# The order of the closing waits on the SP queue of a SwiGLU kernel

## The chip, the cores and the metric

The kernel runs on one core of one Trainium2 chip. The metric is the device time of one execution in microseconds, lower is better. Each timed execution also comes with the span of the core, from its first to its last recorded instruction; in the profiled executions the time is 1.8 to 2.0 us longer than the span.

Names: PE is TensorE's matmul pipeline, ACT is ScalarE, DVE is VectorE, POOL is GpSimd, SP is SyncE. SP computes nothing here; it issues most DMAs and does the closing waits. S[102] is semaphore number 102. A DMA raises its semaphore by 16 in sixteen updates; the last of the sixteen is called its landing.

## The reference, cut to what matters

```python
B, S, D, F = 1, 2048, 640, 1536          # all bfloat16
def reference(x, w_gate, w_up, w_down):
    g = jax.nn.silu(x @ w_gate)
    u = x @ w_up
    return (g * u) @ w_down
```

## The kernel before

The kernel works in four blocks of 512 rows: gate and up projection, SiLU on ACT, product on DVE, then the down projection in four pieces of 128 rows. At the start, eight matmuls on constants warm TensorE up while x is being loaded.

```python
    N_WARM = 8
    ...
    def warm(n):
        pw = psum.tile([P, S_BLK], f32, tag="gu", name="pw", bufs=4)
        for _ in range(n):
            nc.tensor.matmul(pw[:], lhsT=ones[:, 0:P], rhs=ones, start=True, stop=True)
    warm(N_WARM)
    ... # then the first blocks of x are transposed (pt), and the projections begin
```

The very last piece of output, stored in two parts by two queues:

```python
            nc.scalar.copy(ot[:, 0:DA], po_a[:])
            if not last:
                nc.scalar.copy(ot[:, DA:D], po_b[:])
                nc.sync.dma_start(out=out2[s0 : s0 + P, :], in_=ot[:])
            else:
                nc.sync.dma_start(out=out2[s0 : s0 + P, 0:DA], in_=ot[:, 0:DA])    # L172, raises S[100]
                nc.scalar.copy(ot[:, DA:D], po_b[:])
                nc.scalar.dma_start(out=out2[s0 : s0 + P, DA:D], in_=ot[:, DA:D])  # L174, raises S[102]
```

The end of the program is not in the source: leaving the tile context adds it. SP gets one drain that waits for eleven semaphores (eight of the DMAs, and those of DVE, ACT and POOL). Then comes a barrier of all engines, in which POOL gathers and releases; then POOL clears the semaphores; then comes a second barrier. The compiler does not leave the eleven waits in one instruction. It keeps the first of the list in the drain and puts the other ten into five semaphore-wait instructions ahead of it, paired from the two ends of what is left of the list, the outermost pair last. The built program of before has this order on SP (S[100] to S[108] without 101 are the DMAs, 109 is DVE, 110 ACT, 99 POOL):

```
1  wait   S[104], S[103]
2  wait   S[105], S[102]      <- S[102]: the store L174, the last to land
3  wait   S[106], S[100]      <- S[100]: the store L172
4  wait   S[107], S[109]
5  wait   S[108], S[110]
6  drain  S[99]
7  drain of the first barrier: S[97]==0, then raises S[96], for which POOL waits
```

The Trainium skill (Perfetto Trace Analysis, Identifying Dependency Chains) says that "instructions waiting on multiple engines may have EventSemaphore instructions inserted prior to the instruction with additional wait conditions". This program agrees: five of them were inserted ahead of the drain. Which semaphore lands in which of them is what the change is about.

Of the kernel before, what the change touches and what calls it, by code (L numbers as in the profile page):

```python
# [7 lines left out]


@with_exitstack  # L10
def kernel(
    ctx: ExitStack,
    tc: tile.TileContext,
    x: bass.AP,
# [5 lines left out]
    nc = tc.nc  # L20
# [153 lines left out]
                nc.scalar.dma_start(out=out2[s0 : s0 + P, DA:D], in_=ot[:, DA:D])  # L174


# [1 line left out]
_INS = ['x', 'w_gate', 'w_up', 'w_down']  # L178
_OUTS = [((1, 2048, 640), 'bfloat16')]
# [25 lines left out]
```

## Time and profile before

| | before |
|---|---|
| time, median of 3 runs | 167.04 us (166.79 to 167.18) |
| span of the profiled execution | 165.2 us |
| PE busy | 160.5 us, 97% of the span |
| issue of the last store L174 | 162.560 us |
| landing of S[100] / S[102] | 163.981 / 164.147 us |
| POOL's step of the first barrier | 164.496 us |
| clearing of the semaphores | 164.767 us |

The page of before, its busy times, and its chain of work that ended last:

```profile
PE 160.5 (97%) x890; PEld 80.3 (49%) x907; DVE 34.9 (21%) x52; ACT 43.5 (26%) x81; POOL 0.7 (0%) x6
...
PE 97%; issue 1%; DVE 0%; ACT 0%
```

TensorE is the limit for nearly the whole span, so the closing waits on SP can matter only in the tail, which is a different stage. The timeline of ACT from 161.5 us on (start, duration, what) shows where computing stops, and the DMA issues of the window from 162 to 165 us (size, then issue to landing in us) show what comes after it:

```profile
162.26 0.27 ACT L173 CAST ot<-po_b 128x128 bf16<-128x128 f32 x1
162.56 0.36 ACTq L174 DMA_DIRECT2D out_dram<-ot  x1
```

```profile
out_dram<-ot SPq DMA_DIRECT2D x1, 128.0 KB, 1.7
out_dram<-ot ACTq DMA_DIRECT2D x1, 32.0 KB, 1.6
```

From 162.56 us on, the core waits 1.6 us for a store of 32 KB and then closes down. The view of the source line to which the end of the program belongs (L200), SP only, lists its wait instructions with the shortest, median and longest duration in ns and the first and last start:

```profile
L200 SPq EVENT_SEMAPHORE  x7: 17/28/1472, 162.6 to 165.1; - x7
L200 SPq DRAIN  x3: 7/7/13, 164.4 to 164.7; - x3
```

One wait took 1472 ns, the others 17 to 28. That view does not say which one. The single records of the trace do (start in us, duration in ns):

```
162.629    28  SP    EVENT_SEMAPHORE  S[104] S[103]
162.698  1472  SP    EVENT_SEMAPHORE  S[105] S[102]     ends at 164.170
              (S[102] landed at 164.147)
164.204    28  SP    EVENT_SEMAPHORE  S[106] S[100]
164.268    28  SP    EVENT_SEMAPHORE  S[107] S[109]
164.329    28  SP    EVENT_SEMAPHORE  S[108] S[110]
164.394    13  SP    DRAIN            S[99]
164.464     7  SP    DRAIN            S[97]==0, raises S[96]
164.496    17  POOL  EVENT_SEMAPHORE  S[96]>=4
```

The second wait is the decisive one. When it ends, SP still has to walk through four instructions, three waits and a drain, whose conditions have been met (S[100] 0.17 us earlier, the others long before). It arrives at the barrier 0.29 us later, and everyone else is already there.

### The profile page before, as it was taken

How to read it: one execution, taken by the hardware profiler on the slowest of the kernel's cores; microseconds unless marked ns; L12 is line 12 of the kernel's file. 1: busy time of each engine (PE TensorE's matmuls, PEld its weight loads, DVE VectorE, ACT ScalarE, POOL GpSimd, SP SyncE). 2: the span in 40 equal slices, each digit the busy share in tenths (PEclk: the TensorE clock that was granted, in tenths of full speed). 3: DMA queues.
4: the chain of work that ended last, by engine and by line, in shares of the span. 5: the costliest groups of instructions: out<-in, count | busy, mean ns of one | idle time of the engine just before them, and what ended most of it. 6: DMA issues, size and time to landing. Idle time of an engine off the chain costs nothing.

```text
span 165.2 us, 2137 instructions
## 1 busy us (share of the span) xinstructions
PE 160.5 (97%) x890; PEld 80.3 (49%) x907; DVE 34.9 (21%) x52; ACT 43.5 (26%) x81; POOL 0.7 (0%) x6
## 2 busy tenths in 40 slices
PE   8999999999999999999999999999999999999992
PEld 2844444455644444455554444445654444445551
DVE  0433333300013333310003333330002233331000
ACT  3042222222332222223232222222232222222222
POOL 1000000000000000000000000000000000000000
PEclk9999999999999999999999999999999999999999
DMA  5999999801110000001110000001111000000121
GB/s 147 294 326 327 362 230 223 160 29 55 40 40 0 0 4 0 0 0 42 68 55 0 0 2 0 0 4 40 40 40 40 4 0 0 0 0 0 46 78 40
DMA packets 18906, 11.27 MB, mean 68 GB/s; under 512 B 9681, under 2 KB 18897, under 8 KB 18897
## 3 DMA queue, kind: packets, MB, share of 16 engines
q1 hardware_dynamic: 18096, 10.95, 24.2%
q10 hardware_dynamic: 800, 0.20, 0.5%
q8 instruction: 7, 0.11, 0.3%
q14 instruction: 3, 0.02, 0.0%
HBM read 6.55 MB, written 2.62 MB: 56 GB/s over the span
## 4 chain that ended last, share of the span: by engine, by line
PE 97%; issue 1%; DVE 0%; ACT 0%
PE pg L112 31%; PE pu L112 31%; PE po_a L150 25%; PE po_b L159 7%; PE pw L98 2%; PE pt L105 1%; DVE xT L108 0%; ACT ot L173 0%
## 5 line engine op out<-in xcount | busy, mean ns | idle before, releaser
L112 PE MATMUL pg<-xT,wg_sb 128*128 128x512 bf16 (+2 forms) x244 | 59.5, 371 | 0.4
L112 PE MATMUL pu<-xT,wu_sb 128*128 128x512 bf16 (+2 forms) x241 | 59.6, 375 | 0.2
L141 DVE TENSOR_TENSOR aT<-sg,pu 128x512 bf16<-128x512 f32 x48 | 33.0, 687 | 109.2 <-PE pu L112 108.0
L140 ACT ACTIVATE sg<-pg 128x512 f32<-128x512 f32 x48 | 28.7, 597 | 76.2 <-PE pg L112 76.2
L150 PE MATMUL po_a<-wd_sb,aT 128*128 128x512 bf16 x185 | 43.4, 379 | 0.3
L112 PEld LDWEIGHTS <-wu_sb 128*128 128x128 bf16 x245 | 23.7, 98 | 27.9
L112 PEld LDWEIGHTS <-wg_sb 128*128 128x128 bf16 x250 | 24.0, 98 | 27.2 <-issue 0.2
L150 PEld LDWEIGHTS <-aT 128*128 128x128 bf16 x192 | 18.3, 98 | 19.8
L167 ACT CAST ot<-po_a 128x512 bf16<-128x512 f32 x16 | 9.4, 585 | 40.4 <-PE po_a L150 38.0
L159 PEld LDWEIGHTS <-aT 128*128 128x128 bf16 x192 | 12.1, 98 | 3.8
L159 PE MATMUL po_b<-wd_sb,aT 128*128 128x128 bf16 x192 | 13.3, 220 | 0.1
L98 PE MATMUL pw<-const-bfloat16-1.0 128*128 128x512 bf16 x8 | 3.6, 625 | 0.8 <-PEq L189 0.8
L169 ACT CAST ot<-po_b 128x128 bf16<-128x128 f32 x15 | 4.0, 265 | 1.1
L108 DVE COPY xT<-pt 128x640 bf16<-128x640 bf16 x4 | 2.0, 490 | 5.8 <-PE pt L105 5.7
L105 PEld LDWEIGHTS <-x_sb 128*128 128x128 bf16 x20 | 2.0, 133 | 0.6 <-DMA x_sb<-in_x_dram 0.5
L105 PE MATMUL pt<-ident,x_sb 128*128 128x128 bf16 x20 | 2.2, 289 | 0.0
L98 PEld LDWEIGHTS <-const-bfloat16-1.0 128*128 128x128 bf16 x8 | 1.0, 137 | 2.4 <-issue 2.4
L140 ACT ACT_TABLE_LOAD x1 | 1.3, 1283 | 1.3 <-PEq L189 1.3
masks.py:199 POOL TENSOR_SCALAR_AFFINE_SELECT ident<-ident 128x128 bf16<-128x128 bf16 x1 | 0.3, 292 | 0.1
L173 ACT CAST ot<-po_b 128x128 bf16<-128x128 f32 x1 | 0.3, 265 | 0.0
masks.py:197 POOL MEMSET ident<- 128x128 bf16 x1 | 0.2, 204 | 0.3 <-POOLq L189 0.3
L189 POOL MEMSET const-bfloat16-1.0<- 128x1 bf16 x1 | 0.1, 101 | 0.0
(3 smaller groups left out, 0.3 us busy)
## 6 DMA issues: line engine op xcount, KB each, us to landing
out_dram<-ot SPq DMA_DIRECT2D x15, 160.0 KB, 1.8
wd_sb<-in_w_down_dram SPq DMA_DIRECT2D x1, 1920.0 KB, 12.5
wg_sb<-in_w_gate_dram SPq DMA_DIRECT2D x3, 480.0 KB, 7.0
wu_sb<-in_w_up_dram SPq DMA_DIRECT2D x3, 480.0 KB, 7.6
x_sb<-in_x_dram SPq DMA_DIRECT2D x1, 320.0 KB, 3.2
x_sb<-in_x_dram SPq DMA_DIRECT2D x2, 160.0 KB, 3.7
wg_sb<-in_w_gate_dram SPq DMA_DIRECT2D x1, 320.0 KB, 5.0
wu_sb<-in_w_up_dram SPq DMA_DIRECT2D x1, 320.0 KB, 5.5
```

The costliest lines, as they stand in the source:

```text
L98: nc.tensor.matmul(pw[:], lhsT=ones[:, 0:P], rhs=ones, start=True, stop=True)
L105: nc.tensor.transpose(out=pt[:, kd, :], in_=x_sb[:, c, kd * P : (kd + 1) * P], identity=ident[:])
L108: nc.vector.tensor_copy(out=xT[:, :, c * P : (c + 1) * P], in_=pt[:])
L112: nc.tensor.matmul(ps[:, c0:c1], lhsT=w_sb[:, kd, fc * P : (fc + 1) * P], rhs=xT[:, kd, sb * S_BLK + c0 : sb * S_BLK + c1], start=(kd == 0 ...
L140: nc.scalar.activation(sg[:], pg[:], ACT.Silu)
L141: nc.vector.tensor_tensor(out=aT[:, fc, s_sl], in0=sg[:], in1=pu[:], op=ALU.mult)
L150: nc.tensor.matmul(po_a[:], lhsT=aT[:, kf, s0 : s0 + P], rhs=wd_sb[:, kf, 0:DA], start=(kf == 0), stop=(kf == KF - 1),)
L159: nc.tensor.matmul(po_b[:], lhsT=aT[:, kf, s0 : s0 + P], rhs=wd_sb[:, kf, DA:D], start=(kf == 0), stop=(kf == KF - 1),)
L167: nc.scalar.copy(ot[:, 0:DA], po_a[:])
L169: nc.scalar.copy(ot[:, DA:D], po_b[:])
L173: nc.scalar.copy(ot[:, DA:D], po_b[:])
L189: nc = _bacc.Bacc("TRN2", target_bir_lowering=False, num_devices=1)
```

## The change

The intent is to put the semaphores that rise last at the end of SP's walk, so that the other waits are done while the last store is still landing. A function goes over the built program, notes for each semaphore the last instruction that raises it, and sorts the waits of the closing drain. The latest goes first in the list, because the compiler keeps the first of the list in the drain, which is executed last.

```diff
+def _wait_for_the_latest_last(nc):
+    raised = {}
+    for block in nc.main_func.blocks:
+        for k, ins in enumerate(block.instructions):
+            s = ins.sync_info
+            for u in (s.on_update if s is not None else []):
+                raised[u.id] = (block.name, k)
+    at = {b.name: n for n, b in enumerate(nc.main_func.blocks)}
+    ... # for each drain with more than two waits:
+                key = lambda w: (at[raised[w.id][0]], raised[w.id][1])
+                block.instructions[k] = mybir.InstDrain(
+                    ...
+                        on_wait=sorted(s.on_wait, key=key, reverse=True),
+                    ...
+                )
+
+def tile_standalone__swiglu_ffn__prompt_kernel(tc, *args):
+    _body(tc, *args)                     # the kernel of before
+    tc.close()
+    tc.compile()
+    _wait_for_the_latest_last(tc.nc)
```

The built program differs from before in SP's six closing instructions and nowhere else:

```
1  wait   S[109], S[106]
2  wait   S[105], S[107]
3  wait   S[104], S[108]
4  wait   S[103], S[100]
5  wait   S[99],  S[110]
6  drain  S[102]
7  drain of the first barrier
```

More of the change, by code (lines that the diff above doesn't have):

```diff
@@ L10, with _body @@
 @with_exitstack
-def kernel(
+def _body(
     ctx: ExitStack,
@@ L174, with kernel @@
                 nc.scalar.dma_start(out=out2[s0 : s0 + P, DA:D], in_=ot[:, DA:D])
+def _wait_for_the_latest_last(nc):
[6 more added lines that the diff above has]
+    at = {b.name: n for n, b in enumerate(nc.main_func.blocks)}
+    for block in nc.main_func.blocks:
+        for k, ins in enumerate(block.instructions):
+            s = ins.sync_info
+            if isinstance(ins, mybir.InstDrain) and s is not None and len(s.on_wait) > 2:
+                key = lambda w: (at[raised[w.id][0]], raised[w.id][1])
+                block.instructions[k] = mybir.InstDrain(
+                    name=ins.name,
+                    engine=ins.engine,
+                    is_reset_sema=ins.is_reset_sema,
+                    debug=ins.debug,
+                    sync_info=mybir.SyncInfo(
+                        on_wait=sorted(s.on_wait, key=key, reverse=True),
+                        on_update=list(s.on_update),
+                    ),
+                )
+def kernel(tc, *args):
+    _body(tc, *args)
+    tc.close()
+    tc.compile()
+    _wait_for_the_latest_last(tc.nc)
 _INS = ['x', 'w_gate', 'w_up', 'w_down']
```

## The prediction

> **What bounds the kernel.** TensorE. The page gives PE busy 97% of a span of 165.2 us at a granted clock of 1.000, and the chain that ended last is 97% PE. The last po_b matmul's result comes at 162.24, the ACT copy L173 runs 162.26 to 162.53, and ACT issues the last store (L174) at 162.56. In the remaining 2.6 us nothing computes: the store lands, then come the closing waits and barriers. The change touches only those.
>
> **The tail, from the records of the end of the program (line L200, SP, and the DMA landings, us):**
> - Store L172 (S[100], issued by SP) has its 16th update at 163.981; store L174 (S[102], issued by ACT) at 164.147. The store before them landed by 161.07.
> - SP goes through five waits of two semaphores each and a drain with one. The second holds S[102]: it starts at 162.698, takes 1472 ns and ends at 164.170, 23 ns after the last landing.
> - Behind it stand waits whose semaphores have long risen: starts 164.204, 164.268, 164.329 (28 ns each), the drain at 164.394 (13 ns), and the barrier's drain at 164.464. Only then POOL goes on (164.496). ACT's own drain had ended at 163.11.
>
> So 0.294 us pass on the critical path from the end of the decisive wait to SP's arrival at the barrier.
>
> **What the change does.** The built programs differ only in these six SP instructions: same count, same semaphores and values, every engine's order the same. New order: DVE and S[106]; S[105], S[107]; S[104], S[108]; S[103], S[100]; POOL and ACT; the drain on S[102]. Nothing is removed or added; waits move ahead of the last landing.
>
> **Cost.** SP reaches the fourth wait early, as 64 ns is such an instruction's pitch. It ends with S[100], about 164.00. The fifth then runs 164.04 to 164.07, and the drain begins about 164.10, 45 ns before S[102] is full. So the S[100] store just does not hinder. The drain should end about 164.17, and the barrier's drain follow 57 ns later (as it did after 164.407), at 164.23 instead of 164.464. Estimated gain 0.23 us, all on the critical path, since SP comes last to the barrier. Without the profiler an instruction may cost less than 64 ns; and where S[100] lands as late as S[102], about 0.1 us comes back. The Trainium skill (DMA: Bandwidth & Descriptors, Anatomy of one DMA) puts most of a DMA's fixed cost of about 2 us in the write receipt; the 1.6 us from issue to landing here agree in kind, and the change leaves them.
>
> **Predicted time.** 167.04 - 0.22 = 166.82 us, a gain of 0.13%. The three runs of before spread over 0.39 us, more than the effect. Range 166.5 to 167.1 (8 in 10). Faster by over 2%: 0.01; within 2%: 0.98; slower by over 2%: 0.01.
>
> **What would show it.** After: SP's wait of 1.5 us no longer stands second. A wait ending with S[100] comes fourth, then a short one, then the drain ending with S[102]; from the 16th update of S[102] to POOL's step 0.35 us before (164.147 to 164.496), about 0.12 after. Everything up to 162.5 us should repeat within its scatter; PE busy, the landings of 1.6 to 1.7 us and the barriers (0.6 us) should not move.
>
> **What would make it wrong.** A waiting drain might wake more slowly than a semaphore wait; S[100] might land after S[102]; or the landing may scatter by over 0.2 us between executions, hiding the gain in the total while the tail's order still shows it.

## The result, and the profile after

The changed kernel took 166.60 us (median of 4 runs, 166.38 to 166.79), the kernel before 166.99 us in the four runs it is compared with. The ratio is 0.9981 with a 95% interval from 0.9963 to 1.0, so within 2%, as forecast. Ratios here are the mean time of one kernel's fast runs over that of the other's of the same rounds, which is not quite the ratio of the medians quoted.

The page of the profile after, busy times and chain:

```profile
PE 159.9 (97%) x890; PEld 79.4 (48%) x907; DVE 34.9 (21%) x52; ACT 43.5 (26%) x81; POOL 0.7 (0%) x6
...
PE 95%; DMA 2%; issue 1%; SPq 0%; ACT 0%
```

The DMA share of this chain is the loading of x at the start, for which the transposes waited in this execution.

The same view of the end of the program (now line L206), SP only:

```profile
L206 SPq EVENT_SEMAPHORE  x7: 17/28/1167, 162.3 to 164.5; - x7
L206 SPq DRAIN  x3: 7/7/13, 163.8 to 164.1; - x3
```

The number of instructions is the same, seven waits and three drains. Only the longest wait has changed, from 1472 to 1167 ns. The single records show why:

```
162.307    28  SP    EVENT_SEMAPHORE  S[109] S[106]
162.376    28  SP    EVENT_SEMAPHORE  S[105] S[107]
162.438    28  SP    EVENT_SEMAPHORE  S[104] S[108]
162.502  1167  SP    EVENT_SEMAPHORE  S[103] S[100]     ends at 163.669 (S[100] landed at 163.648)
163.704    28  SP    EVENT_SEMAPHORE  S[99]  S[110]
              (S[102] landed at 163.815)
163.830    13  SP    DRAIN            S[102]
163.900     7  SP    DRAIN            S[97]==0, raises S[96]
163.932    17  POOL  EVENT_SEMAPHORE  S[96]>=4
```

From the landing of S[102] to POOL's step it is 163.932 - 163.815 = 0.117 us, where before had 164.496 - 164.147 = 0.349. That is the predicted gain of 0.23 us. From POOL's step to the end of the span nothing has changed: 165.154 - 164.496 = 0.658 us before, 164.590 - 163.932 = 0.658 after.

But the spans differ by 165.154 - 164.590 = 0.564 us, more than twice the gain in the tail. The rest was there before the tail began: the last store was issued at 162.241 us instead of 162.560. The page's two lines for the warm-up and the transposes at the start (count, busy us, mean ns of one) show where it arose. Before:

```profile
L98 PE MATMUL pw<-const-bfloat16-1.0 128*128 128x512 bf16 x8 | 3.6, 625 | 0.8 <-PEq L189 0.8
L105 PE MATMUL pt<-ident,x_sb 128*128 128x128 bf16 x20 | 2.2, 289 | 0.0
```

After:

```profile
L98 PE MATMUL pw<-const-bfloat16-1.0 128*128 128x512 bf16 x8 | 3.3, 589 | 0.8 <-PEq L222 0.8
L105 PE MATMUL pt<-ident,x_sb 128*128 128x128 bf16 x20 | 1.6, 220 | 0.4 <-DMA x_sb<-in_x_dram 0.2
```

In the profile of before, fifteen of the twenty transposes ran at about 311 ns each and the last five at 219; after, nearly all ran at 219. TensorE came to its full pace later in the one execution than in the other. The change cannot reach that, so it looks like scatter between executions; repeated profiles below test it.

### The profile page after: what moved, and what is told of

It reads as the page before. It is cut to its first block, busy times and chain, and to the rows that moved or that the text cites. A ratio compares the mean times of both kernels' runs of the same rounds, so it can differ in the third digit from the quotient of the medians.

```text
span 164.6 us, 2137 instructions
## 1 busy us (share of the span) xinstructions
PE 159.9 (97%) x890; PEld 79.4 (48%) x907; DVE 34.9 (21%) x52; ACT 43.5 (26%) x81; POOL 0.7 (0%) x6
## 4 chain that ended last, share of the span: by engine, by line
PE 95%; DMA 2%; issue 1%; SPq 0%; ACT 0%
PE pg L112 31%; PE pu L112 31%; PE po_a L150 25%; PE po_b L159 7%; DMA x_sb<-in_x_dram 2%; PE pt L105 0%; SPq L73 0%; ACT ot L173 0%
## 5 line engine op out<-in xcount | busy, mean ns | idle before, releaser
L105 PE MATMUL pt<-ident,x_sb 128*128 128x128 bf16 x20 | 1.6, 220 | 0.4 <-DMA x_sb<-in_x_dram 0.2
L105 PEld LDWEIGHTS <-x_sb 128*128 128x128 bf16 x20 | 1.2, 98 | 1.2 <-DMA x_sb<-in_x_dram 1.2
```

Of the source, the lines that this page charges most:

```text
L105: nc.tensor.transpose(out=pt[:, kd, :], in_=x_sb[:, c, kd * P : (kd + 1) * P], identity=ident[:])
```

## The experiments

Two theories stand against each other.

- **Order theory.** What counts is how many SP instructions stand behind the decisive wait. Each costs about 0.06 us, and the total follows in full, because SP is the last to reach the barrier.
- **Rivals.** The gain in the total is scatter of the start. Or the satisfied waits cost nothing in the total. Or it is their number on SP that counts and not their order. Or what matters is which semaphore shares an instruction with which, or that the decisive wait is a drain.

The common edit of all experiments but two (the change itself and the kernel before, repeated as they stand) replaces the sorting key by an explicit list, so that any order can be built.

```diff
-                        on_wait=sorted(s.on_wait, key=key, reverse=True),
+                        on_wait=[by[n] for n in ORDER],
```

Below, "tail" is the time from the landing of S[102] to POOL's step of the first barrier. All results were correct. The runs shared three chips: the change again, the decisive wait first and the twelve behind and ahead ran on one; the decisive wait fifth, the other store last, the barrier's own drain and the waits on POOL on another; the two exchanged and the kernel before, once more, on a third.

### The change again

No edit: the changed kernel, five rounds.

> The change once more, in five rounds. Order theory: from the last landing to POOL's barrier step 0.117 us (before 0.349), so the total lies 0.23 us under before, a ratio of 0.9986. Rival, scatter of the start: the first records gained 0.32 us before the tail began (the last store's issue at 162.24 against 162.56), from the landings of x; if that was all, five rounds give a ratio between 0.999 and 1.001.

Measured: 166.74 us against 166.97, ratio 0.9984 (0.9967 to 1.0002). The tail is 0.118 us. This profile answers the rival directly: its last store was issued at 162.772 us, 0.21 us later than in the profile of before, and its span is nevertheless no longer (the view of the cores):

```profile
core 0: 165.1 us, clock 1.000
```

The late start gave back what the tail had won. In the one profile the scatter added to the gain, in the other it cancelled it; the tail was the same in both. The expectation had put the early start of the first profile down to the landings of x. That was wrong: x took 3.4 to 3.9 us from issue to landing there and 3.2 to 3.7 in before, so it landed later, not earlier. The ratio lies near the forecast of 0.9986, but this run's interval alone does not shut out 1.

### The decisive wait first

```diff
+1  wait   S[102], S[100]
+2  wait   S[108], S[107]
+3  wait   S[106], S[105]
+4  wait   S[104], S[103]
+5  wait   S[109], S[110]
+6  drain  S[99]
```

> Same six instructions, but the waits for the two last stores stand in the first, so five SP instructions follow the last landing instead of four in before and none in after. Order theory: 0.349 + 0.064 = 0.41 us from last landing to POOL's step, total 0.06 us over before, which the total can hardly show but the tail does. Rival, that what helped is S[100] and S[102] standing apart or which engine's semaphore shares a wait: no step of 64 ns for one place.

Measured: ratio 1.0003 (0.9989 to 1.0018), tail 0.429 us. One more instruction behind the landing made the tail longer than before's 0.349, by 0.080 instead of 0.064; a later run explains part of this. S[100] and S[102] share a wait here, which is no help.

### Twelve satisfied waits behind

```diff
+ORDER: the order of before, then twelve waits of (S[109], S[99]), then the drain on S[99]
```

> The order of before with twelve more waits for semaphores that rose long ago, behind the decisive one: sixteen SP instructions after the last landing. Order theory: 0.349 + 12 x 0.064 = 1.12 us from last landing to POOL's step, total 0.77 us over before (ratio 1.0046), above the noise. Rival, that satisfied waits cost nothing in the total (hidden by a later step of the end): total as before within 0.2 us.

Measured: 167.82 us against 166.97, ratio 1.0046 (1.0030 to 1.0063), about 0.77 us slower (0.0046 x 167). The tail is 1.073 us, so twelve waits added 1.073 - 0.349 = 0.724 us, 60 ns each. Waits for semaphores that rose more than ten microseconds earlier (DVE's last operation ends near 150 us) cost full time when they stand behind the last landing.

### The same twelve ahead

```diff
+ORDER: twelve waits of (S[109], S[99]), then the order of the change
```

> The same instructions as in the run with twelve behind, same number, in the order of the change with the twelve ahead of all: SP has them done by about 163.6 of the span of before, ahead of the landings. Order theory: 0.117 us from last landing to POOL's step, total 0.23 us under before and 1.0 us under the twelve behind, although SP executes twelve instructions more than either kernel. Rival, that the number of SP instructions counts: 0.5 us or more over before.

Measured: 166.63 us, ratio 0.9980 (0.9966 to 0.9994), tail 0.107 us. These two kernels have the same waits, multiplied alike, in the same number of instructions. Their views of the end of the program (SP, 162 to 165.4 us) have the same kinds of lines. With the twelve behind:

```profile
L207 SPq EVENT_SEMAPHORE  x17: 27/28/1462, 162.7 to 165.1; - x17
```

With the twelve ahead (the window also holds the two waits of the barriers, hence 19):

```profile
L207 SPq EVENT_SEMAPHORE  x19: 17/28/442, 162.2 to 164.4; - x19
```

Ahead, the twelve take time out of the long wait, which shrinks to 442 ns; behind, they stand after a wait of 1462 ns. The medians on the same chip differ by 167.82 - 166.63 = 1.19 us (forecast 1.0; the tails alone give 1.073 - 0.107 = 0.966). So the number of instructions does not count, and their order does. The tail is 10 ns shorter than the change's because the drain's record took 7 ns instead of 13 and the next followed after 59 ns instead of 70. Why it did so is open.

### The decisive wait fifth, the drain trivial

```diff
-5  wait   S[99],  S[110]
-6  drain  S[102]
+5  wait   S[102], S[110]
+6  drain  S[99]
```

> Order of the change, but S[102] in the fifth wait and POOL's long risen semaphore in the drain. Order theory: one instruction follows the decisive wait, 0.117 + 0.06 = 0.18 us from last landing to POOL's step. Rival, that a drain is woken later than a wait: under 0.15 us, no loss against the change. In the total 0.06 us, too little to see.

Measured: tail 0.182 us, against 0.117 with the drain. So the drain was not woken later than the wait (records 15 and 16 ns after the landing); what counts is the one instruction more. The total, ratio 0.9982 (0.9968 to 0.9997), cannot tell the two apart, as was said beforehand.

### The other store last

```diff
-4  wait   S[103], S[100]
-6  drain  S[102]
+4  wait   S[103], S[102]
+6  drain  S[100]
```

> Order of the change with the two last stores exchanged: the drain waits for S[100] (SP's store, landed 0.17 us earlier in both profiles), the fourth wait for S[102]. Order theory: two instructions follow the decisive wait, 0.117 + 2 x 0.06 = 0.24 us, half of the gain given back. Rival, that it is enough to have both last stores late in the order: 0.12 us as in the change.

Measured: tail 0.212 us, ratio 0.9993 (0.9979 to 1.0008). About half of the gain is gone: 0.137 us of 0.232 remain in the tail. Late in the order is not enough; the wait that ends last has to stand last. The change sorts by the place in the program, not by landing. Here the two agree: S[102] landed 0.166 or 0.167 us after S[100] in every one of the twelve profiles.

### The two of one wait exchanged

In before and in the run with the other store last, S[102] is the second of the two semaphores of its wait; in the runs with it first and fifth, it is the first. This run differs from the run with the decisive wait fifth in that alone.

```diff
-5  wait   S[102], S[110]
+5  wait   S[110], S[102]
```

> The run with S[102] in the fifth wait had it as the first of the two semaphores: its record began 16 ns after the landing, took 28 ns, and the next instruction stood 81 ns after the landing. In before and in the run with the stores exchanged S[102] was the second: the record held the waiting, ended 23 ns after the landing, and the next instruction stood 57 ns after it. Here the two in the fifth wait change places, nothing else. If the place within the wait makes that difference: 0.18 - 0.024 = 0.158 us from last landing to POOL's step and a long record. If it came from other neighbours: 0.18 us.

Measured (one look): tail 0.162 us, against 0.182. The records of the fifth wait (start, duration), first with S[102] as its first semaphore, then as its second:

```
164.155    28  SP    EVENT_SEMAPHORE  S[102] S[110]     S[102] landed at 164.139
164.220    13  SP    DRAIN            S[99]             81 ns after the landing

164.149   132  SP    EVENT_SEMAPHORE  S[110] S[102]     S[102] landed at 164.258
164.318    13  SP    DRAIN            S[99]             60 ns after the landing
```

Waiting for the second semaphore is part of the record and waiting for the first is not; the next instruction comes 21 ns sooner after the second. All profiles agree: the next instruction starts 57 to 62 ns after the landing where S[102] is the second (five profiles) and 81 or 86 where it is the first (two). This has the right sign for both misses, the 16 ns too many with the decisive wait first and the 28 ns too few with the other store last. It is not their whole size: in both of those runs the instruction after the closing drain also came 12 ns sooner than in before or the change (58 instead of 70 ns), for a reason that stays open.

### The wait in the barrier's own drain

```diff
-6  drain  S[102]
-7  drain of the first barrier: S[97]==0, raises S[96]
+6  drain  S[97]==0
+7  drain of the first barrier: S[102], raises S[96]
```

> The wait for S[102] moved into the barrier's own drain on SP, whose wait (the barrier's release semaphore at zero) goes to the closing drain just ahead. Order theory: no instruction between the landing and SP's arrival, 0.117 - 0.06 = 0.055 us to POOL's step, total 0.29 us under before. If a drain that waits needs its 57 ns before it signals anyway: 0.12 us.

Measured: tail 0.050 us, the shortest with the wait on SP. The ratio, 0.9982 (0.9965 to 1.0), does not stand out from the change's: 0.07 us is below what these rounds resolve. Its profile, a late start again, even has a span of 165.2 us.

### The waits on POOL, ahead of the clearing

Which instruction really needs the stores to have landed? The end of the program does, and before it POOL, which clears the semaphores that the stores still have to raise. The first barrier need not wait for them, as this run tries out.

```diff
 SP:    waits for S[103] to S[108], S[99], S[109], S[110]; first barrier
-       and for S[100], S[102]
 POOL:  first barrier: gathers, releases
+       wait  S[100]
-       drain
+       drain S[102]
        clears the semaphores; second barrier
```

> The waits for both last stores taken from SP to POOL's drain between the two barriers, ahead of the clearing of the semaphores, so that the first barrier runs during the landing. Order theory taken further: from the last landing to the clearing 0.62 us in before, 0.39 in after, here about 0.10 to 0.13; to the end of the span 1.01, 0.78 and about 0.5; total 0.5 us under before (ratio 0.997). If the first barrier is not what stands there, or POOL's drain wakes slowly: total no better than the change.

Measured: 166.42 us against 166.99, ratio 0.9968 (0.9954 to 0.9982), the lowest ratio. POOL's step of the first barrier now stands at 163.045 us, 0.994 us ahead of the landing. From the landing to the clearing it takes 0.130 us (before 0.620, after 0.388), to the end of the span 0.517 us (1.007 and 0.775). The two views of the end of the program, SP and POOL, from 162 us on:

```profile
L222 SPq EVENT_SEMAPHORE  x6: 17/28/28, 162.5 to 164.5; - x6
...
L222 POOLq EVENT_SEMAPHORE  x5: 17/17/17, 163.0 to 164.4; - x5
L222 POOLq DRAIN  x2: 34/56/77, 164.1 to 164.3; - x2
L222 POOLq EVENT_SEMAPHORE_RANGE_CLEAR  x1: 96/96/96, 164.2 to 164.2; - x1
```

SP has no long wait any more. It still cannot leave early, since the second barrier holds every engine until POOL has cleared the semaphores. The results were correct; nothing else on record checks that this order is safe. This kernel is faster than before. That it also beats the change is shown by the stage, 0.775 - 0.517 = 0.258 us from the landing to the end of the span, and not by the totals: the two did not run in the same rounds, and though both ratios are against before and differ by (0.9984 - 0.9968) x 167 = 0.27 us, their intervals overlap.

### The kernel before, once more

> The kernel before, profiled once more, to see how far its tail repeats: order theory, 0.34 to 0.36 us from last landing to POOL's step whatever the total; the issue of the last store may lie anywhere between 162.2 and 162.9.

Measured (one look): tail 0.349 us, as in the first profile to the nanosecond. The single time was 166.72 us, as low as the change's median; another execution of this kernel on the same chip took 167.14. Its start was a quick one:

```profile
L105 PE MATMUL pt<-ident,x_sb 128*128 128x128 bf16 x20 | 1.6, 220 | 0.4 <-DMA x_sb<-in_x_dram 0.4
```

### All together

"Behind" counts SP's instructions between the decisive wait and the barrier's drain. The last two columns compare with before: how much sooner after the landing the span ended, and what the ratio means at 167 us.

| kernel | behind | tail, us | landing to end, us | against before's 1.007 | (ratio - 1) x 167 |
|---|---|---|---|---|---|
| twelve behind | 16 | 1.073 | 1.730 | +0.72 | +0.77 |
| decisive first | 5 | 0.429 | 1.086 | +0.08 | +0.05 |
| before | 4 | 0.349 | 1.007 | 0 | 0 |
| other store last | 2 | 0.212 | 0.869 | -0.14 | -0.12 |
| fifth, not the drain | 1 | 0.182 | 0.840 | -0.17 | -0.30 |
| the change, again | 0 | 0.118 | 0.775 | -0.23 | -0.27 |
| twelve ahead | 0 | 0.107 | 0.764 | -0.24 | -0.33 |
| in the barrier's drain | none, the barrier's own | 0.050 | 0.708 | -0.30 | -0.30 |
| on POOL | not on SP | | 0.517 | -0.49 | -0.53 |

Over a range of 1.2 us the total follows the tail within 0.13 us, although the interval of each single ratio reaches some 0.25 us to either side (0.0015 x 167).

And the start, from the twelve profiles, in the order of the time at which the trace records the full clock granted to TensorE. Both columns are us from the span's start:

| profile | full clock granted at | last store issued at |
|---|---|---|
| after | 3.71 | 162.241 |
| before, once more | 3.73 | 162.323 |
| twelve ahead | 3.82 | 162.098 |
| decisive first | 4.87 | 162.480 |
| on POOL | 5.08 | 162.465 |
| fifth, not the drain | 5.29 | 162.559 |
| the change, again | 5.72 | 162.772 |
| other store last | 5.79 | 162.559 |
| before | 5.93 | 162.560 |
| the two exchanged | 6.08 | 162.682 |
| twelve behind | 6.21 | 162.651 |
| in the barrier's drain | 6.66 | 162.871 |

Both kernels are found early and late. An early grant goes with an early last store, and from the first three rows to the rest lie about 0.4 us, nearly twice the effect of the change. That the grant causes it was not tested by an experiment; it fits the transposes, which run at 311 ns before it and 219 after.

## Why the prediction was right or wrong

**The size and the total: right.** Forecast 166.82 us with a range from 166.5 to 167.1, a gain of 0.22. Measured 166.60 in the first comparison and 166.74 in the second, with gains from the ratios of 0.32 and 0.27 us. The total alone does not prove it: both intervals reach 1, and with about 0.3 us to either side, more than the gain itself, it is partly luck that both gains came out within 0.1 us of the forecast. The size rests on the tail, and on the twelve ahead, which have the same order behind the landing and whose interval (0.9966 to 0.9994) does shut out 1.

**The mechanism: right, and shown.** "From the 16th update of S[102] to POOL's step 0.35 us before (164.147 to 164.496), about 0.12 after": 0.349 and 0.117. Moving the decisive wait from fifth-last to last of the six changed the tail as the count of instructions says, with twelve waits more as well as with one, and the same twelve ahead of it cost nothing.

**The S[100] store "just does not hinder": right.** The fourth wait ended at 163.669 us and the fifth's record at 163.732, 83 ns ahead of S[102]. The prediction had 45 ns between the drain's start and the landing; when the drain itself began to wait the record does not tell, as it starts only after the landing.

**"A waiting drain might wake more slowly": it did not.** Its record began 15 ns after the landing; replacing it by a wait made the tail longer.

**"S[100] might land after S[102]": not seen.** S[102] was last in all twelve profiles. The Trainium skill (DMA: Bandwidth & Descriptors, Two DMAs through the same engine are not ordered) says that "Nothing at all orders DMAs across the 16 engines", so this order is an observation; no run here shows it turned around. What it would cost was measured: the run with the other store last.

**The source of the noise: not where it was feared.** The prediction feared that "the landing may scatter by over 0.2 us between executions". As the time from the issue of the last store to its landing it did not: 1.56 to 1.59 us in all twelve profiles. The moment of the landing did scatter (163.68 to 164.46 us), but from what lies ahead of it: the last store was issued between 162.10 and 162.87 us, and most of that goes with the moment at which TensorE gets its full clock, between 3.7 and 6.7 us. "Everything up to 162.5 us should repeat within its scatter" was thus true, but the size of that scatter was not stated. It is 0.77 us, more than three times the effect, and one pair of profiles read by their spans would have made the change look worth 0.56 us.

**Where the store's time goes.** The records of its packets split these 1.6 us, the same way in all twelve profiles: 0.88 to 0.89 us from the issue to the first data packet, 0.27 to 0.30 while the data packets run, and 0.40 to 0.41 from the end of the last data packet to the landing.

**Left open.** Every timed run comes with a recorded span, so no run here tells what a satisfied wait costs without the profiler's records. Why the closing drain sometimes takes 7 and sometimes 13 ns is open as well.

## What to carry to other kernels

When the only thing left at the end is a store's landing, look at what stands behind the wait for it. Here every instruction behind it on SP, the engine that reached the barrier last, was paid in full, even if its own condition was met long before: 60 ns each. Put the wait that ends last behind all others, or better on the instruction that really needs it, so that barriers run while the store lands. For an effect of a tenth of a per cent, compare the stage that the change touches from a landmark inside it, and don't trust two spans: here more than half of the difference arose before the tail began.

## What the Trainium skill lacked or had wrong

- Perfetto Trace Analysis, Sequencer-only Instruction (DRAIN, etc): it says that the profiler reports the execution only and the semaphore wait not at all. That holds here for drains (the record of the drain on S[102] begins 15 ns after the landing) and for the first of a wait instruction's two semaphores (16 ns after the landing, 28 ns long). It does not hold for the second semaphore: with the two exchanged the record took 132 ns and ended 23 ns after the landing, and in before the record was 1472 ns long, nearly all of it waiting. The next instruction followed 60 instead of 81 ns after the landing.
- Perfetto Trace Analysis, Identifying Dependency Chains: it mentions the inserted wait instructions, but not that their order counts. Here one cost 60 ns behind the last landing (twelve added 0.724 us) and nothing ahead of it.
- TensorE: Matmul & The Clock Gate, Part 1: The HAM clock gate: it puts the run-to-run scatter of the moment of the full clock at 500 ns to either side. A note in the same section allows for more, as one kernel there had 6, 11 or 14 slow matmuls. Here the larger scatter was seen. The full clock came 3.7 to 6.7 us after the span's start, with the first matmul at 0.77 us, so 2.9 to 5.9 us after it; in the two profiles of before alone it came at 5.9 and 3.7 us. The page speaks of sustained matmul activity, and in the two quick starts shown above TensorE stood idle for 0.4 us at the transposes. The moment goes with most of the scatter of the last store's issue here.
- No page has the closing waits and barriers that leaving the tile context adds to a kernel: from POOL's step of the first barrier to the end of the span it took 0.658 us here, and the wait for the last stores could be moved behind the first barrier, which took 0.258 us off the time from landing to end.
